# Convolution and gated feed-forward: lanes that convolve one unit ahead instead of two

## The chip, the cores and the metric

The kernel runs on one core of one Trainium2 chip. The metric is device time in microseconds of one execution. The core has five engines with queues of their own: PE (TensorE), DVE (VectorE), ACT (ScalarE), POOL (GpSimd) and SP (SyncE, which here issues DMAs and transposes). In the profile, PEld is TensorE's weight load, and a name such as POOLq is an engine's queue.

## The reference

The input x has 8 sequences of 4096 tokens with 192 channels, in float32. Each of 8 heads (24 channels) is convolved causally over 7 tokens with a softmax of 7 weights, and every token then passes a feed-forward layer of width 1536 with a product of two branches:

```python
w = softmax(weight)                                   # [8, 7], one set of taps per head
x_pad = concatenate([zeros(B, 6, D), x], axis=1)
y[b, s, h, :] = sum(w[h, k] * x_pad[b, s + k, h, :] for k in range(7))
y = y.reshape(B * S, 192)
out = (maximum(y @ w_gate, 0) * (y @ w_val)) @ w_out  # w_gate, w_val [192, 1536], w_out [1536, 192]
```

## The kernel before

Two sequences, b and b + 4, are handled side by side: one on partitions 0 to 63, the other on 64 to 127. The 192 channels are three groups c of 64. The work goes in 16 units u of 1024 tokens (of two sequences each), and each unit has two windows of 512 tokens.

A unit has two phases on TensorE. In the gate phase `gate_val(u, w)` is called for both windows. For each of 12 slices f of the width it issues six matmuls with Wg and six with Wv (L505), which read `xc[u]`, the convolved tokens. ScalarE takes the gate through a ReLU (L516, tile gr), and VectorE multiplies it by the value branch in PSUM (L517, tile hT). In the projection phase `project(u, ...)` multiplies hT by Wo for four outputs of 512 tokens each, i = 0 to 3, each in two turns of half height (`half_pass`, L539). The first unit uses matmuls of full height instead (`half_whole`, L559). `evict` copies each output out of PSUM (L576): ScalarE alone, and for i = 3 ScalarE and VectorE half each, except in unit 0. The PSUM pool has four buffers, used in turn, so the value matmuls of the second slice in a gate phase take the buffer that output i = 3 held.

The convolution is done in three ways:

- Unit 0: on TensorE with banded matrices, straight into `xc[0]` (`conv_dense`, L333).
- Unit 1: on TensorE too (`conv`, L358), in two calls of two parts, then copied by ScalarE to a tile y (L373) and transposed by DMAs of SP's queue into `xc[1]` (L395). The second call sits inside unit 0's projection.
- Units 2 to 15: "lanes". `lane_load` (L414) loads the tokens, `lane_turn` has GpSimd reorder them (L433, tile x_p) and SP's queue transpose them in nine DMAs (L436, tile x_r). Then each tap is a multiplication by a scalar per partition and an addition. Tokens 0 to 575 of the unit are VectorE's: ScalarE makes the first tap's product (`lane_first`, L469, tile acc), and VectorE accumulates the other six taps for three channel groups, 18 instructions (`lane_rest`, L481), of which the last three write `xc`. Tokens 576 to 1023 are made as 21 products (`product`, L452 on ScalarE, L454 on VectorE, tile prods), and GpSimd sums them in six adds (`add`, L458), the last of which writes `xc`. `VECTOR` lists the products (c, k) that VectorE makes; the rest are ScalarE's, spread over the four outputs of a projection (`work`, `cut`).

The order in each engine's queue is the order in which the program is written (`manual_schedule`); semaphores between engines are set by tile regions. In the loop over u, the products and accumulations for unit u + 2 are issued in unit u's projection, and the adds for unit u + 1 in unit u's gate phase, around `lane_turn(u + 2)` and `lane_load(u + 3)` in GpSimd's queue:

```python
lane = 1 <= u < NUNIT - 1
if lane:
    add(u + 1, 1)
...
if u + 2 < NUNIT:
    lane_first(u + 2)
    lane_rest(u + 2)
```

The tiles acc, prods and x_p have one buffer each, x_r two, xc three.

Of the kernel before, what the change touches and what calls it, by code (L numbers as in the profile page):

```python
# [15 lines left out]
def kernel(  # L16
# [23 lines left out]
    WIN = 512  # L40
    NWIN = S // WIN
    SUB = 112
    VECTOR = [
        [(0, 5), (1, 5), (2, 5), (0, 4), (1, 4), (2, 4), (2, 1)],
        [(0, 5), (1, 5), (2, 5), (0, 6), (2, 1)],
    ]
# [10 lines left out]
    GROUPS = [(0, [DSUB * j for j in range(GSUB)]), (0, [WIN + DSUB * j for j in range(GSUB)])]  # L57
    second = [min(t, 2 * UNIT - SUB) for t in range(UNIT, 2 * UNIT, SUB)]
    GROUPS += [(0, second[:GSUB]), (0, second[GSUB:])]
# [3 lines left out]
    xpool = ctx.enter_context(tc.tile_pool(name="xpool", bufs=3))  # L63
# [3 lines left out]
    ypool = ctx.enter_context(tc.tile_pool(name="ypool", bufs=2))  # L67
# [7 lines left out]
    def load_x(g):  # L75


        bp, toks = GROUPS[g]
        xt = xpool.tile([128, GSUB, 2, D], F16, name="x_h")
        rows, step = (SUB, DSUB) if g < 2 else (128, SUB)  # L80
        for st in range(2):
            b = bp + NB * st
            last = toks[-1] - toks[-2] != step
            n_full = len(toks) - int(last)
            src = bass.AP(
                tensor=x.tensor,
                offset=x.offset + (b * S + toks[0] - PAD) * D,
                ap=[[D, rows], [step * D, n_full], [1, D]],
            )
            nc.gpsimd.dma_start(out=xt[0:rows, 0:n_full, st, :], in_=src)  # L90
            if last:
                nc.gpsimd.dma_start(
                    out=xt[0 : SUB + PAD, len(toks) - 1, st, :],
                    in_=x[b, toks[-1] - PAD : toks[-1] + SUB, :],
                )
        return xt
# [208 lines left out]
    PLACE = {0: (0, 0, 0), 1: (0, 0, 1), 3: (0, 1, 0), 4: (0, 1, 1)}  # L305
    PLACE |= {6: (1, 0, 0), 7: (1, 0, 1), 2: (1, 1, 0), 5: (1, 1, 1)}

    def conv_dense(g, c):


        xt = xts[g]
        if g == 0 and c == 0:
            xc[0] = xcpool.tile([128, NCH, UNIT], F16, name="xc")
            both_halves(nc.vector.tensor_copy, 0, Wg)
            both_halves(nc.vector.tensor_copy, 0, Wv)
        t0 = GROUPS[g][1][0]
        rows = ROWS0
        ps = psum.tile([128, 2, 512], FP, name="ps")
        late = (1, 2, 3, 4, 0)
        both = [(jj, (0, 1)) for jj in late]  # L320
        if g == 0 and c == 0:
            both = [(jj, (st,)) for st in range(2) for jj in late[0:4]] + both[4:]
        for jj, sts in both:
            col = DSUB * jj
            n = min(DSUB, WIN - col)
            for second in range(2):
                for st in sts:
                    for k2 in range(2):
# [4 lines left out]
                        nc.tensor.matmul(  # L333
                            out=ps[p0 : p0 + m, 0, col : col + n],
                            lhsT=xt[0:rows, jj, st, 32 * k : 32 * k + m],
                            rhs=band(h)[0:rows, 0:n],
                            start=True,
                            stop=True,
                            tile_position=(0, p0),
                            skip_group_check=True,  # L340
                        )
# [3 lines left out]
    convs = {}  # L345

    def conv(g, part):


        xt = xts[g]  # L350
        bp, toks = GROUPS[g]
        n = len(toks)
        rows = SUB + PAD
        W = 2 * n * G
        ps = psum.tile([128, 2, 512], FP, name="ps")
        for h, (t, bank, slot) in PLACE.items():
            if t == part:
                nc.tensor.matmul(  # L358
                    out=ps[0:SUB, bank, W * slot : W * (slot + 1)],
                    lhsT=band(h),  # L360
                    rhs=xt[0:rows, 0:n, :, G * h : G * (h + 1)],
                    start=True,
                    stop=True,
                    skip_group_check=True,
                )
        if part == 0:
            convs[g] = ypool.tile([128, GSUB, NCH, 2, 64], F16, name="y")
        y = convs[g]

        def move(copy, bank, i0, step_in, c, r0, step_out, width):  # L370
            src = ps[0:SUB, bank, 0 : 2 * W]
            dst = y[0:SUB, 0:n, 0, :, 0:1]
            copy(  # L373
                out=bass.AP(
                    tensor=dst.tensor,
                    offset=dst.offset + 128 * c + r0,
                    ap=[dst.ap[0], [step_out, 2], [NCH * 128, n], [64, 2], [1, width]],
                ),
                in_=bass.AP(
                    tensor=src.tensor,  # L380
                    offset=src.offset + i0,
                    ap=[src.ap[0], [W + step_in, 2], [2 * G, n], [G, 2], [1, width]],
                ),
            )

        if part == 0:
            move(nc.scalar.copy, 0, 0, 0, 0, 0, G, G)
            move(nc.scalar.copy, 1, 0, 0, 1, 8, G, G)
            return
        move(nc.scalar.copy, 0, 0, 0, 2, 16, G, G)  # L390
        move(nc.scalar.copy, 1, 0, 8, 0, 48, 2 * 128 - 48, 16)
        move(nc.scalar.copy, 1, 16, -16, 1, 0, 56, 8)
        for jj, t in enumerate(toks):
            u, k = t // UNIT, min(SUB, UNIT - t % UNIT)
            nc.sync.dma_start_transpose(  # L395
                out=xc[u][:, :, t % UNIT : t % UNIT + k],
                in_=y[0:k, jj].rearrange("p c s r -> p (c s r)"),
            )
# [78 lines left out]
    def lane_rest(u):  # L477
# [11 lines left out]
        for c, k in VECTOR[u > 2]:  # L489
            product(nc.vector, u, c, k)  # L490
# [65 lines left out]
    def half_whole(h, st, outs):  # L556
        for q in range(4):
            for f in range(NFF):
                nc.tensor.matmul(  # L559
                    out=outs[q],  # L560
                    lhsT=h[:, f, st, 128 * q : 128 * (q + 1)],
                    rhs=Wo[:, f, :],
                    start=(f == 0),
                    stop=(f == NFF - 1),
                )

# [30 lines left out]
    def project(u, hs, work):  # L597
# [3 lines left out]
        if u == 0:  # L601
            order = [(i, 2) for i in range(4)]
        if u == NUNIT - 1:
            order = [(0, 0), (1, 0), (0, 1), (2, 0), (1, 1), (2, 3), (3, 0), (2, 4), (3, 1)]
        for i, turn in order:
            final = u == NUNIT - 1 and i == 3
            h, st = hs[i // 2], i % 2
            if turn in (0, 2):
                at[i] = slots(final)
            if turn in (1, 2):  # L610
                for c, k in work[i]:
                    product(nc.scalar, u + 2, c, k)
# [12 lines left out]
            if turn == 2:  # L625
                half_whole(h, st, at[i][1])
            else:
                done[i] = half_pass(h, st, at[i][1], final, turn, done.get(i))
            if turn:
                evict(at[i][0], (bp + NB * st) * S + WIN * (w0 + i // 2), final, u > 0 and i == 3)  # L630
            if u == 0 and i == 0:
                conv(3, 0)
                conv(3, 1)
# [9 lines left out]
    lane_load(2)  # L643
    xts[2] = load_x(2)
    nc.gpsimd.dma_start(out=Wo[:], in_=moe_w_out.rearrange("(c p) d -> p c d", p=128))
    for u in range(NUNIT):
        lane = 1 <= u < NUNIT - 1
        if lane:
            add(u + 1, 1)
        if u == 1:  # L650
            lane_load(3)
            add(2, 2)
            add(2, 3)
        hs = []
        if u == 0:
            hs.append(gate_val(0, 0))
        if u + 2 < NUNIT:
            lane_turn(u + 2)
        if u == 0:
            xts[3] = load_x(3)  # L660
        if 0 < u < NUNIT - 3:
            lane_load(u + 3)
        if lane:
            for k in range(4 if u == 1 else 2, KW - 1):
                add(u + 1, k)
        while len(hs) < 2:
            hs.append(gate_val(u, len(hs)))
        if lane:
            add(u + 1, KW - 1)
        if u == 0:  # L670
            xc[1] = xcpool.tile([128, NCH, UNIT], F16, name="xc")
            conv(2, 0)
            conv(2, 1)
        del xc[u]
        work = [[] for _ in range(4)]
        if u + 2 < NUNIT:
            lane_first(u + 2)
            lane_rest(u + 2)
# [35 lines left out]
```

## Time and profile before

| what | value |
|---|---|
| time, median of 3 runs | 768.64 us (768.06 to 768.94) |
| span of the profiled execution | 767.4 us |
| PE busy | 761.4 us, 99% |
| DVE busy | 692.2 us, 90% |
| ACT busy | 601.7 us, 78% |
| POOL busy | 369.9 us, 48% |
| L505 gate and value matmuls, mean of one | 376 ns, 4608 of them |
| L539 projection matmuls, mean of one | 243 ns, 5760 of them |
| L517 multiply on DVE | 1216 ns, 386 of them |
| L481 accumulation on DVE | 815 ns, 252 of them |
| L458 add on POOL | 3035 ns, 84 of them |

The profiler records a span from the first to the last instruction; a time of its own for the profiled execution is not given, and the median of the timed runs lies 1.2 us above that span. The share of an engine's busy time is an average over both phases of a unit. PE's matmuls overlap, since two of half height run at once and the next is issued before the last has ended, so a mean duration is not the distance from one to the next; for that the chain and the timeline are read. The granted TensorE clock is full in all 40 slices of the span.

### The profile page before, as it was taken

How to read it: one execution, taken by the hardware profiler on the slowest of the kernel's cores; microseconds unless marked ns; L12 is line 12 of the kernel's file. 1: busy time of each engine (PE TensorE's matmuls, PEld its weight loads, DVE VectorE, ACT ScalarE, POOL GpSimd, SP SyncE). 2: the span in 40 equal slices, each digit the busy share in tenths (PEclk: the TensorE clock that was granted, in tenths of full speed). 3: DMA queues.
4: the chain of work that ended last, by engine and by line, in shares of the span. 5: the costliest groups of instructions: out<-in, count | busy, mean ns of one | idle time of the engine just before them, and what ended most of it. 6: DMA issues, size and time to landing. Idle time of an engine off the chain costs nothing.

```text
span 767.4 us, 24881 instructions
## 1 busy us (share of the span) xinstructions
PE 761.4 (99%) x10842; PEld 502.1 (65%) x10842; DVE 692.2 (90%) x745; ACT 601.7 (78%) x736; POOL 369.9 (48%) x212
## 2 busy tenths in 40 slices
PE   9999999999999999999999999999999999999997
PEld 4495674946649476584855848567494674947657
DVE  7999999999999999999999999999999999995590
ACT  6797887878888788888878878788787887874671
POOL 8608648093570926619165290843809355080000
PEclk9999999999999999999999999999999999999999
DMA  8956727180462705428064271722719131200202
GB/s 121 138 97 118 91 90 88 54 122 6 100 78 69 107 23 98 59 85 94 26 112 43 85 91 44 109 28 89 89 50 110 21 95 37 65 21 23 63 2 85
DMA packets 131827, 56.13 MB, mean 73 GB/s; under 512 B 96757, under 2 KB 131717, under 8 KB 131717
## 3 DMA queue, kind: packets, MB, share of 16 engines
q1 hardware_dynamic: 90805, 38.85, 24.9%
q0 software_dynamic: 40768, 15.59, 18.8%
q8 instruction: 85, 1.39, 0.8%
q14 instruction: 25, 0.20, 0.1%
q10 hardware_dynamic: 144, 0.10, 0.0%
HBM read 31.68 MB, written 25.17 MB: 74 GB/s over the span
## 4 chain that ended last, share of the span: by engine, by line
PE 99%; DMA 1%; issue 0%; DVE 0%; POOL 0%; POOLq 0%
PE ps L505 65%; PE ps L539 31%; PE ps L559 2%; DMA x_h<-in_x_dram 1%; PE ps L333 0%; PE ps L358 0%; DVE acc L576 0%; POOL spaced L129 0%; POOLq L698 0%
## 5 line engine op out<-in xcount | busy, mean ns | idle before, releaser
L517 DVE TENSOR_TENSOR hT<-gr,ps 128x1024 f16<-128x1024 f16 (+1 forms) x386 | 469.0, 1216 | 36.9 <-ACT gr L516 9.9
L516 ACT ACTIVATE gr<-ps 128x1024 f16<-128x1024 f32 (+1 forms) x386 | 393.3, 1020 | 101.9 <-PE ps L505 100.1
L458 POOL TENSOR_TENSOR prods<-prods 128x1344 f32<-128x1344 f32 x70 | 212.5, 3035 | 309.8 <-DVE prods L454 306.4
L505 PE MATMUL ps<-xc,Wg 64*128 64x512 f16 x2304 | 311.9, 376 | 0.0
L505 PE MATMUL ps<-xc,Wv 64*128 64x512 f16 x2304 | 311.8, 376 | 0.0
L539 PEld LDWEIGHTS <-hT 64*128 64x128 f16 x5760 | 238.0, 94 | 3.6
L539 PE MATMUL ps<-Wo,hT 64*128 64x192 f16 x5760 | 240.1, 243 | 0.0
L505 PEld LDWEIGHTS <-Wv 64*128 64x128 f16 x2304 | 129.6, 94 | 118.7 <-DVE hT L517 0.3
L505 PEld LDWEIGHTS <-Wg 64*128 64x128 f16 x2304 | 112.2, 94 | 132.5 <-issue 0.5
L481 DVE SCALAR_TENSOR_TENSOR acc<-x_r,tap,acc 128x576 f32<-128x576 f16 x210 | 154.3, 815 | 1.6 <-DMA x_r<-x_p 1.6
L452 ACT ACTIVATE prods<-x_r,tap 128x448 f32<-128x448 f16 x222 | 130.4, 664 | 0.0
L576 ACT COPY out_s<-ps 128x768 f32<-128x768 f32 (+1 forms) x64 | 46.2, 722 | 53.9 <-PE ps L539 44.0
L414 POOL DMA_DIRECT2D x_e<-in_x_dram x56 | 45.2, 818 | 3.3 <-POOL x_p L433 3.3
L433 POOL COPY x_p<-x_e 128x1728 f16<-128x1728 f16 x28 | 44.8, 1627 | 1.5 <-DMA x_e<-in_x_dram 1.5
L458 POOL TENSOR_TENSOR xc<-prods 128x1344 f16<-128x1344 f32 x14 | 42.4, 3026 | 1.1
L481 DVE SCALAR_TENSOR_TENSOR xc<-x_r,tap,acc 128x576 f16<-128x576 f16 x42 | 31.8, 816 | 0.0
L469 ACT ACTIVATE acc<-x_r,tap 128x576 f32<-128x576 f16 x42 | 29.4, 768 | 0.0
L454 DVE TENSOR_SCALAR prods<-x_r,tap 128x448 f32<-128x448 f16 x72 | 27.4, 452 | 0.0
L576 DVE COPY out_s<-ps 128x384 f32<-128x384 f32 x14 | 7.8, 556 | 14.8 <-ACT out_s L576 14.8
L559 PE MATMUL ps<-Wo,hT 128*128 128x192 f16 x192 | 16.2, 246 | 0.0
L559 PEld LDWEIGHTS <-hT 128*128 128x128 f16 x192 | 15.9, 98 | 0.0
L576 DVE COPY acc<-ps 128x192 f32<-128x192 f32 x1 | 0.4, 358 | 14.2 <-PE ps L539 14.2
(52 smaller groups left out, 62.6 us busy)
## 6 DMA issues: line engine op xcount, KB each, us to landing
out_dram<-out_s SPq DMA_DIRECT2D x62, 384.0 KB
x_e<-in_x_dram POOLq DMA_DIRECT2D x34, 192.0 KB, 6.2
x_e<-in_x_dram POOLq DMA_DIRECT2D x22, 240.0 KB, 5.0
x_r<-x_p SPq DMA_TRANSPOSE x126
Wo<-in_moe_w_out_dram POOLq DMA_DIRECT2D x1, 576.0 KB
x_h<-in_x_dram POOLq DMA_DIRECT2D x2, 240.0 KB, 7.3
x_h<-in_x_dram POOLq DMA_DIRECT2D x2, 210.0 KB, 4.7
x_h<-in_x_dram POOLq DMA_DIRECT2D x2, 192.0 KB, 7.7
```

Source lines behind the costliest of these rows:

```text
L414: nc.gpsimd.dma_start(out=xe[:, j : j + n, st, :, :].rearrange("p j c r -> p j (c r)"), in_=bass.AP(tensor=x.tensor, offset=x.offset + (b ...
L433: nc.gpsimd.tensor_copy(out=xp[:, :, :, st, :], in_=xe[:, :, st, :, :])
L452: engine.activation(out=out, in_=in_, func=ACTF.Copy, scale=scale)
L458: nc.gpsimd.tensor_tensor(out=pr[:, 0] if k < KW - 1 else xc[u][:, :, LDVE:UNIT], in0=pr[:, 0], in1=pr[:, k], op=ALU.add,)
L469: nc.scalar.activation(out=accs[u][:, c, :], in_=shifted(u, c, 0, 0), func=ACTF.Copy, scale=tap[:, c, 0:1],)
L481: nc.vector.scalar_tensor_tensor(out=xc[u][:, c, 0:LDVE] if k == KW - 1 else acc[:, c, :], in0=shifted(u, c, k, 0), scalar=tap[:, c, k : k ...
L505: nc.tensor.matmul(out=pss[i][:, st, :], lhsT=W[64 * st : 64 * st + 64, c, 128 * f : 128 * (f + 1)], rhs=xcb[64 * st : 64 * st + 64, c, WI ...
L516: nc.scalar.activation(out=gr[:, sts], in_=pss[0][:, sts], func=ACTF.Relu)
L517: nc.vector.tensor_tensor(out=h[:, f, sts], in0=gr[:, sts], in1=pss[1][:, sts], op=ALU.mult)
L539: mm = nc.tensor.matmul(out=outs[q], lhsT=h[64 * r : 64 * r + 64, f, st, 128 * q : 128 * (q + 1)], rhs=Wo[64 * r : 64 * r + 64, f, :], sta ...
L559: nc.tensor.matmul(out=outs[q], lhsT=h[:, f, st, 128 * q : 128 * (q + 1)], rhs=Wo[:, f, :], start=(f == 0), stop=(f == NFF - 1),)
L576: one(out=dst[:, step * j : step * j + step], in_=src[:, step * j : step * j + step])
```

## The change

The lanes now make unit u + 1 in unit u, not unit u + 2, and unit 1 is made by them as well. `conv` and its tile y are gone, with the loads of x for it; `half_whole` is gone, so that unit 0 projects as the others do, and its last output too is copied by ScalarE and VectorE. All six adds stand behind `project` in the program, so that in GpSimd's queue they follow `lane_turn(u + 1)` and `lane_load(u + 2)` and wait only for the products. `VECTOR` is one list of five products; the product (2, 1) goes to ScalarE and (1, 6) to VectorE.

```diff
-    VECTOR = [
-        [(0, 5), (1, 5), (2, 5), (0, 4), (1, 4), (2, 4), (2, 1)],
-        [(0, 5), (1, 5), (2, 5), (0, 6), (2, 1)],
-    ]
+    VECTOR = [(0, 5), (1, 5), (2, 5), (0, 6), (1, 6)]
...
-    xpool = ctx.enter_context(tc.tile_pool(name="xpool", bufs=3))
+    xpool = ctx.enter_context(tc.tile_pool(name="xpool", bufs=2))
...
-    ypool = ctx.enter_context(tc.tile_pool(name="ypool", bufs=2))
...
-    def conv(g, part):
...
-        for c, k in VECTOR[u > 2]:
+        for c, k in VECTOR:
             product(nc.vector, u, c, k)
...
-    def half_whole(h, st, outs):
...
     def project(u, hs, work):
...
-        if u == 0:
-            order = [(i, 2) for i in range(4)]
...
-                    product(nc.scalar, u + 2, c, k)
+                    product(nc.scalar, u + 1, c, k)
...
-                evict(at[i][0], (bp + NB * st) * S + WIN * (w0 + i // 2), final, u > 0 and i == 3)
-            if u == 0 and i == 0:
-                conv(3, 0)
-                conv(3, 1)
+                evict(at[i][0], (bp + NB * st) * S + WIN * (w0 + i // 2), final, i == 3)
...
-    lane_load(2)
-    xts[2] = load_x(2)
+    lane_load(1)
     nc.gpsimd.dma_start(out=Wo[:], in_=moe_w_out.rearrange("(c p) d -> p c d", p=128))
     for u in range(NUNIT):
-        lane = 1 <= u < NUNIT - 1
-        if lane:
-            add(u + 1, 1)
-        if u == 1:
-            lane_load(3)
-            add(2, 2)
-            add(2, 3)
+        lane = u + 1 < NUNIT
         hs = []
         if u == 0:
             hs.append(gate_val(0, 0))
+        if lane:
+            lane_turn(u + 1)
         if u + 2 < NUNIT:
-            lane_turn(u + 2)
-        if u == 0:
-            xts[3] = load_x(3)
-        if 0 < u < NUNIT - 3:
-            lane_load(u + 3)
-        if lane:
-            for k in range(4 if u == 1 else 2, KW - 1):
-                add(u + 1, k)
+            lane_load(u + 2)
         while len(hs) < 2:
             hs.append(gate_val(u, len(hs)))
-        if lane:
-            add(u + 1, KW - 1)
-        if u == 0:
-            xc[1] = xcpool.tile([128, NCH, UNIT], F16, name="xc")
-            conv(2, 0)
-            conv(2, 1)
         del xc[u]
         work = [[] for _ in range(4)]
-        if u + 2 < NUNIT:
-            lane_first(u + 2)
-            lane_rest(u + 2)
+        if lane:
+            lane_first(u + 1)
+            lane_rest(u + 1)
             todo = [(c, k) for k in (0, 1, 2, 3, 4, 6) for c in range(NCH)]
-            todo = [ck for ck in todo if ck not in VECTOR[u > 0]]
-            cut = [0, 4, 8, 12, 16] if u == 0 else [0, 5, 10, 15, 16]
-            work = [todo[a:b] for a, b in zip(cut, cut[1:])]
+            todo = [ck for ck in todo if ck not in VECTOR]
+            work = [todo[a:b] for a, b in zip([0, 5, 10, 15], [5, 10, 15, 16])]
         project(u, hs, work)
+        if lane:
+            for k in range(1, KW):
+                add(u + 1, k)
```

More of the change, by code (lines that the diff above doesn't have):

```diff
@@ L56 @@
     TDVE = (LDVE + HALO) // 128
-    GROUPS = [(0, [DSUB * j for j in range(GSUB)]), (0, [WIN + DSUB * j for j in range(GSUB)])]
-    second = [min(t, 2 * UNIT - SUB) for t in range(UNIT, 2 * UNIT, SUB)]
-    GROUPS += [(0, second[:GSUB]), (0, second[GSUB:])]
+    STARTS = [[DSUB * j for j in range(GSUB)], [WIN + DSUB * j for j in range(GSUB)]]
     ctx.enter_context(tc.manual_schedule())
     const = ctx.enter_context(tc.tile_pool(name="const", bufs=1))
-    xpool = ctx.enter_context(tc.tile_pool(name="xpool", bufs=3))
+    xpool = ctx.enter_context(tc.tile_pool(name="xpool", bufs=2))
     epool = ctx.enter_context(tc.tile_pool(name="epool", bufs=1))
@@ L75, in load_x @@
     def load_x(g):
-        bp, toks = GROUPS[g]
         xt = xpool.tile([128, GSUB, 2, D], F16, name="x_h")
-        rows, step = (SUB, DSUB) if g < 2 else (128, SUB)
         for st in range(2):
-            b = bp + NB * st
-            last = toks[-1] - toks[-2] != step
-            n_full = len(toks) - int(last)
             src = bass.AP(
                 tensor=x.tensor,
-                offset=x.offset + (b * S + toks[0] - PAD) * D,
-                ap=[[D, rows], [step * D, n_full], [1, D]],
-            )
[L90 to L95, printed above, removed]
+                offset=x.offset + (NB * st * S + STARTS[g][0] - PAD) * D,
+                ap=[[D, SUB], [DSUB * D, GSUB], [1, D]],
+            )
+            nc.gpsimd.dma_start(out=xt[0:SUB, :, st, :], in_=src)
         return xt
@@ L301 @@
     xc = {}
-    PLACE = {0: (0, 0, 0), 1: (0, 0, 1), 3: (0, 1, 0), 4: (0, 1, 1)}
-    PLACE |= {6: (1, 0, 0), 7: (1, 0, 1), 2: (1, 1, 0), 5: (1, 1, 1)}
     def conv_dense(g, c):
@@ L315, in conv_dense @@
             both_halves(nc.vector.tensor_copy, 0, Wv)
-        t0 = GROUPS[g][1][0]
+        t0 = STARTS[g][0]
         rows = ROWS0
@@ L343, in conv_dense @@
         copy(out=xc[0][:, c, t0 : t0 + WIN], in_=ps[:, 0, :])
-    convs = {}
-    def conv(g, part):
[L350 to L398, printed above, removed]
     xes, xrs, accs, prods = {}, {}, {}, {}
@@ L554, in half_pass @@
             return done
-    def half_whole(h, st, outs):
[L557 to L565, printed above, removed]
     def put(copy, queue, src, row, n, gap, os_=None):
@@ L607, in project @@
             h, st = hs[i // 2], i % 2
-            if turn in (0, 2):
+            if turn == 0:
                 at[i] = slots(final)
-            if turn in (1, 2):
+            if turn == 1:
                 for c, k in work[i]:
-                    product(nc.scalar, u + 2, c, k)
+                    product(nc.scalar, u + 1, c, k)
             if turn > 2:
@@ L624, in project @@
                 continue
[L625 to L628, printed above, removed]
+            done[i] = half_pass(h, st, at[i][1], final, turn, done.get(i))
             if turn:
-                evict(at[i][0], (bp + NB * st) * S + WIN * (w0 + i // 2), final, u > 0 and i == 3)
-            if u == 0 and i == 0:
-                conv(3, 0)
-                conv(3, 1)
+                evict(at[i][0], (bp + NB * st) * S + WIN * (w0 + i // 2), final, i == 3)
     for c in range(NCH):
```

## The prediction

> **What bounds the kernel now.** I read the page's chain first, then the timeline of one unit in the middle of the run, then the groups behind it.
>
> ```profile
> PE 99%; DMA 1%; issue 0%; DVE 0%; POOL 0%; POOLq 0%
> by line: PE ps L505 64.9%; PE ps L539 31.0%; PE ps L559 2.1%; DMA x_h<-in_x_dram 0.7%; PE ps L333 0.4%; PE ps L358 0.2%; issue 0.1%; DVE acc L576 0.0%; POOL spaced L129 0.0%; POOLq L698 0.0%
> ```
>
> TensorE never waits: the span is its work. So an edit gains only what it takes from TensorE, and loses all by which it makes TensorE wait. In the same chain every later unit is 31.08 us of gate and value matmuls (L505) and 15.84 us of projection (L539), 46.92 us in all. The timeline of one projection, with P = 230.94 us for its start:
>
> ```profile
> 228.96 3.81 DVE L517 TENSOR_TENSOR hT<-gr,ps 128x1024 f16<-128x1024 f16 x3
> 230.94 16.00 PE L539 MATMUL ps<-Wo,hT 64*128 64x192 f16 x384
> 232.69 11.02 DVE L481 SCALAR_TENSOR_TENSOR acc<-x_r,tap,acc 128x576 f32<-128x576 f16 x15
> 237.78 2.91 ACT L452 ACTIVATE prods<-x_r,tap 128x448 f32<-128x448 f16 x5
> 241.74 2.90 ACT L452 ACTIVATE prods<-x_r,tap 128x448 f32<-128x448 f16 x5
> 243.63 2.27 DVE L481 SCALAR_TENSOR_TENSOR xc<-x_r,tap,acc 128x576 f16<-128x576 f16 x3
> 245.82 1.90 DVE L454 TENSOR_SCALAR prods<-x_r,tap 128x448 f32<-128x448 f16 x5
> 246.78 0.81 PE L505 MATMUL ps<-xc,Wg 64*128 64x512 f16 x6
> 247.63 0.55 DVE L576 COPY out_s<-ps 128x384 f32<-128x384 f32 x1
> 247.89 3.03 POOL L458 TENSOR_TENSOR prods<-prods 128x1344 f32<-128x1344 f32 x1 [21.72 <-DVE prods L454]
> ```
>
> The columns are start, length, engine, line, tiles and count. VectorE is busy through the whole projection: 18 accumulations (L481) from P+1.75, 0.735 us apart, five products, and half an eviction that ends at P+17.24. GpSimd stands idle until all of that is done. Its adds (L458) run only in the gate phase, beside the multiplies L517:
>
> ```profile
> L458 POOL TENSOR_TENSOR prods<-prods x70: 3018/3028/3098, 60.7 to 682.6; 128x1344 f32<-128x1344 f32 x70
> L481 DVE SCALAR_TENSOR_TENSOR acc<-x_r,tap,acc x210: 809/814/821, 44.8 to 665.2; 128x576 f32<-128x576 f16 x105
> L517 DVE TENSOR_TENSOR hT<-gr,ps x19: 1220/1221/1223, 201.8 to 225.1; 128x1024 f16<-128x1024 f16 x19
> L517 DVE TENSOR_TENSOR hT<-gr,ps x24: 1220/1221/1223, 699.5 to 745.1; 128x1024 f16<-128x1024 f16 x24
> ```
>
> The last two lines are the multiplies with adds beside them (201 to 226 us) and with GpSimd idle (700 to 746): no nanosecond of difference. But a multiply has one operand in SBUF (gr), the other in PSUM. An accumulation has two in SBUF (x_r, acc), and none of the 252 in this trace runs beside an add.
>
> **The change, part by part.**
>
> *TensorE's convolution of the second unit goes.* In the chain its two pieces are 0.99 and 0.82 us: 1.81 us gained. Its ten ScalarE copies, ten transposes on SP's queue and six GpSimd loads go too; nothing waited for them. The first unit's projection turns from 192 whole-height matmuls (3.96 + 11.88 = 15.84 us) into 384 half-height ones, 15.84 us in every other unit: nothing.
>
> *One more unit goes through the lanes.* Unit 1's takes in unit 0's projection the place that unit 2's had. There VectorE had waited 1.63 us for x_r (44.79 us) and the projection now starts 0.9 us sooner, at about 41.4; the chain ends 44.79 + 15.5 = 60.3 us, TensorE wants it at 41.4 + 17.8 = 59.2: 1.1 us lost once if x_r lands no sooner, 0 if it does. I take 1.1.
>
> *The lanes lose a unit of lead.* The next unit's first gate matmul now waits for xc that VectorE writes in the projection just before it, its second window for GpSimd's last add. Undisturbed, the first third of xc is there at P+13.5 (243.63 + 0.81) and is wanted at P+15.84; the last third is there at P+14.96 and is wanted four matmuls later, at about P+16.3. The half eviction, behind the five products in VectorE's order, frees the PSUM buffer of the fourth value matmul group: there at P+17.24, wanted at P+17.78 (248.72 us). So the margin is 0.54 us, and every later microsecond of VectorE is one of TensorE.
>
> *GpSimd's queue.* The adds move from the gate phase into the projection: the product (2,1) that held the first one back is now ScalarE's, first of its second five, done at about P+7.5. Adds 1 to 4 need ScalarE's products alone, all there by P+13.7; add 5 needs three of VectorE's, add 6 the last two. Moved behind them are the two turns (L433, 3.2 us), four loads (3.3 us) and, through these, the nine transposes on SP's queue (12.2 us). Undisturbed, six adds take 18.5 us and end at P+26, window 1 opens at P+31.4, and x_r lands at about P+43, before the next projection at P+46.9. All of that is covered, by 5.4 and by 4 us.
>
> *The unknown: an add beside an accumulation.* At P+7.5 the eighth accumulation runs and ten are to come. Bounds: the multiplies say 0 per add; two engines that take strict turns cost VectorE a whole add each, 3.03 us. I take the upper end, because the multiply's row differs in the one thing that matters, the second SBUF operand, and because GpSimd is short of reads itself: its add takes 2.25 ns an element with two operands, its copy x_p 0.94 with one (1629 ns for 1728). With turns, add 1 runs at P+7.65, one accumulation, add 2, one, add 3, one, add 4, then seven: four adds, 12.1 us. Add 5 arrives while the fourth product runs and holds back the fifth. A product is one SBUF operand, but it takes 0.38 us for 448 elements, 0.85 ns each against 1.19 in the multiply and 1.28 in the accumulation: faster than one stream gives on this engine, so it too seems to use a second path. 0 or 3.03; I take 3.03.
>
> The Trainium skill (SBUF — State Buffer, section Who interferes with whom) has a rule against this change: a VectorE instruction with two SBUF inputs contends with a GpSimd instruction that reads SBUF, and the later one waits until the other has finished. No run yet shows it; by it the sum is the one that I take, by the multiplies' row it would be 767.9.
>
> VectorE then ends 5 x 3.03 = 15.15 us later, and TensorE waits 15.15 - 0.54 = 14.6 us in each of 15 units. Nothing gives it back: in the gate phase TensorE needs 1.295 us for each of 24 steps and VectorE 1.22, so behind the wait TensorE sets the pace again. GpSimd is done at about P+35 and the next projection starts at P+61.5, so x_r is in time.
>
> *TensorE after a wait.* It stands from P+15.8 to P+25.7, and again for 4 us. At the program's start it issued its 512-column matmuls every 0.425 us for 3 us, later every 0.216; after 0.64 us of idleness at 5.3 us it was not slow. So 0 to 1.5 us per unit; I take 0, as the waits inside a unit are nearer to the short idleness, and keep 15 x 1.5 = 22 us for the range. The Trainium skill (TensorE: Matmul & The Clock Gate, Part 1) says that the clock halves after about 3.4 us of idleness for about as long; by that rule an estimate of 1.7 us per unit would make it 1012. The trace shows half speed only at the start.
>
> Sum, against the profiled span of 767.4 us (the median of 768.64 has 1.2 us more around it): -1.8 + 1.1 + 15 x 14.6 = +218, so 768.6 + 218 = 987 us. Without add 5's cost it is 15 x 11.6 = 174, 942; with the slow restart 1009.
>
> **Rivals.**
>
> *The adds wait, not VectorE.* Accumulations start every 0.735 us and last 0.814, so they overlap, and GpSimd may find no gap. Then add 1 starts at about P+15 (behind the accumulations) or P+16.7 (behind the products), six take 18.5 us, and window 1, due at P+31.4, opens at P+33.6 to P+35.3: 2.2 to 3.9 us a unit, 33 to 59 us, 801 to 827. For it: the overlap. Against it: a read that ends before its instruction leaves a gap.
>
> *They share.* Both slow down, and VectorE loses half an add each: 6 to 7.5 us, less 0.54, 15 times: 850 to 873. For it: an add at 2.25 ns an element can't fill a path at every cycle. Against: nothing in the trace shows a half-slowed row.
>
> *No collision.* Adds and accumulations run as adds and multiplies do. Then only 1.8 us of TensorE go, less 0 to 1.1: 766.8 to 767.9. It decides as long as VectorE loses under 0.54 us a unit, 0.13 us per overlapped add; the multiplies speak for it, the second operand against.
>
> That the change does not do what it says can be left out: in the built order the first gate matmuls wait for VectorE in three steps, and those of window 1 for GpSimd.
>
> **How the numbers follow.** Turns 0.58, sharing 0.12, waiting adds 0.18, no collision 0.12. The forecast's own range is 942 to 1009. The range leaves out only no collision: from 800, the waiting adds' lower end, to 1015, slow restarts included. About 0.2% (1.5 us) is what a measurement of this kernel can tell from no change. The first three cases are slower: 0.88. No collision is split evenly by unit 0's loss: faster 0.06, same 0.06.
>
> **What would show it.** Right: L481 in the projection with a few instructions of about 3.8 us, or gaps of 3 us in VectorE there; TensorE waiting some 10 us for xc and 4 us for the eviction at each unit's start; units of 61.5 us; about 15 us of projection-phase GpSimd work. Waiting adds: L481 at 814 ns, L458 lengthened, the wait in front of window 1 on GpSimd. Wrong: both lines as before and TensorE still at 99%. Slower restarts would show as the gate phase longer than 31.08 us, free of waits.

## The result and the profile after

The changed kernel takes 856.72 us (median of 5 runs, 856.23 to 858.11) against 768.64: the ratio is 1.1146, with a 95% interval of 1.1134 to 1.1159. That is 88 us slower, where the forecast had 218. The sign was right. The engine that is late was not: the forecast had TensorE wait for VectorE, and it waits for GpSimd. The case that came is the rival in which the adds wait, and one term that the forecast took as zero is added to it.

The page of the changed kernel: the granted clock, the chain, and two groups (busy time and mean ns of one, idle time before them and what ended it).

```profile
PEclk9998999989999899998999989999899998999989
...
PE 75%; POOL 11%; issue 9%; DMA 2%; SPq 1%; ACT 1%; POOLq 0%; DVE 0%; ACTq 0%
...
L384 POOL TENSOR_TENSOR prods<-prods 128x1344 f32<-128x1344 f32 x75 | 361.2, 4816 | 281.9 <-ACT prods L378 277.1
...
L431 PE MATMUL ps<-xc,Wg 64*128 64x512 f16 x2304 | 334.8, 395 | 55.0 <-POOL xc L384 55.0
```

Where TensorE was 99% of the chain, it is 75%; GpSimd and the "issue" time around its adds stand in for the rest. TensorE waits 55.0 us for `xc`, all of it for GpSimd's part and none for VectorE's. The clock, full in every slice before, is below 0.9 in eight of the 40 slices. The adds (now L384) have a mean of 4.8 us instead of 3.03. The next view tells where that mean is from: the lines of the adds and of the accumulations (now L407) over the whole run, as min/median/max ns.

```profile
L384 POOL TENSOR_TENSOR prods<-prods x75: 3018/3025/12067, 50.0 to 810.7; 128x1344 f32<-128x1344 f32 x75
L407 DVE SCALAR_TENSOR_TENSOR acc<-x_r,tap,acc x225: 808/812/816, 43.0 to 793.6; 128x576 f32<-128x576 f16 x113
```

No accumulation is touched (816 ns at most, 821 before), nor a product of VectorE (L380, 453 ns at most). The adds are unchanged in the median, but the longest takes 12.07 us, and that is the first one of a unit. The timeline of one projection, P = 200.23 us:

```profile
200.23 16.01 PE L465 MATMUL ps<-Wo,hT 64*128 64x192 f16 x384
201.98 11.02 DVE L407 SCALAR_TENSOR_TENSOR acc<-x_r,tap,acc 128x576 f32<-128x576 f16 x15
207.83 24.48 POOL L384 TENSOR_TENSOR prods<-prods 128x1344 f32<-128x1344 f32 x5 [19.15 <-ACT prods L378]
212.92 2.27 DVE L407 SCALAR_TENSOR_TENSOR xc<-x_r,tap,acc 128x576 f16<-128x576 f16 x3
215.11 1.90 DVE L380 TENSOR_SCALAR prods<-x_r,tap 128x448 f32<-128x448 f16 x5
...
232.39 3.01 POOL L384 TENSOR_TENSOR xc<-prods 128x1344 f16<-128x1344 f32 x1
...
235.45 1.46 PE L431 MATMUL ps<-xc,Wg 64*128 64x512 f16 x6 [3.67 <-POOL xc L384]
```

Five adds with no gap take 5 x 3.03 + 4 x 0.08 = 15.5 us; here they take 24.48. Add 1 is let go at P+7.60, inside the run of accumulations, and ends 12.06 us later, at 219.89 us. An add's own length of 3.02 us back from there is 216.87, when VectorE's last product was just ending (215.11 + 1.90 = 217.01): as if it had begun only then. From there six adds in a row end at P+35.2. TensorE could have begun window 1 at P+31.4 (24 groups of six matmuls, 0.6475 us apart, from 216.07 us) and is 3.84 us late.

That is not all of the loss: the six matmuls behind the wait take 1.46 us instead of 0.82. Windows of time around the same wait, TensorE alone (length, busy time and matmuls, granted clock, DMA share, GB/s):

```profile
core 0: us, PE busy (x), PEclk, DMA share, GB/s
229.20:235.45 6.25, 2.58 (x24) 0.98 0.00 0
235.45:236.50 1.05, 1.05 (x6) 0.50 0.00 0
...
237.50:238.50 1.00, 1.00 (x8) 0.50 0.00 0
238.50:239.50 1.00, 1.00 (x12) 0.92 0.00 0
239.50:240.50 1.00, 1.00 (x14) 1.00 0.48 98
```

In finer windows of this trace the granted clock is 0.50 from 235.25 to 238.66 us, 3.2 us of it behind the wait. In the next unit it is 0.50 from 286.45 to 293.27 us, 5.5 us of it behind a wait as long (3.66 us), and so in turn through the run. In the chain, the 144 matmuls that follow take 17.28 or 18.4 us, in turn from unit to unit, instead of the 15.72 that the same piece takes at full clock (`e11_fill`, below):

```profile
235.45 17.28 PE ps L431 x144
...
287.77 18.41 PE ps L431 x144
```

So a unit loses 3.84 us to the adds and 1.6 or 2.7 us to the clock. Units of 46.92 us have become 52.3 and 53.4 us.

### The profile page after: what moved, and what is told of

It is laid out like the page before. It is cut to its first block, busy times and chain, and to the rows that moved or that the text cites. A ratio compares the mean times of both kernels' runs of the same rounds, so it can differ in the third digit from the quotient of the medians.

```text
span 854.5 us, 25310 instructions
## 1 busy us (share of the span) xinstructions
PE 795.2 (93%) x11018; PEld 526.5 (62%) x11018; DVE 706.5 (83%) x767; ACT 609.4 (71%) x747; POOL 523.9 (61%) x218
## 4 chain that ended last, share of the span: by engine, by line
PE 75%; POOL 11%; issue 9%; DMA 2%; SPq 1%; ACT 1%; POOLq 0%; DVE 0%; ACTq 0%
PE ps L431 50%; PE ps L465 25%; POOL xc L384 5%; POOL prods L384 5%; SPq L362 1%; DMA x_e<-in_x_dram 1%; DMA Wg<-in_moe_w_gate_dram 1%; ACT prods L378 1%; DMA x_r<-x_p 0%; POOLq L600 0%; POOL Wg L164 0%; POOL Wg L157 0%; POOL x_e L340 0%; ACT out_s L491 0%; POOL Wv L157 0%
## 5 line engine op out<-in xcount | busy, mean ns | idle before, releaser
L384 POOL TENSOR_TENSOR prods<-prods 128x1344 f32<-128x1344 f32 x75 | 361.2, 4816 | 281.9 <-ACT prods L378 277.1
L431 PE MATMUL ps<-xc,Wg 64*128 64x512 f16 x2304 | 334.8, 395 | 55.0 <-POOL xc L384 55.0
L431 PE MATMUL ps<-xc,Wv 64*128 64x512 f16 x2304 | 331.5, 391 | 0.0
L465 PEld LDWEIGHTS <-hT 64*128 64x128 f16 x6144 | 254.3, 94 | 3.5
L465 PE MATMUL ps<-Wo,hT 64*128 64x192 f16 x6144 | 256.2, 243 | 0.0
L431 PEld LDWEIGHTS <-Wg 64*128 64x128 f16 x2304 | 128.5, 98 | 191.0 <-issue 80.6
L431 PEld LDWEIGHTS <-Wv 64*128 64x128 f16 x2304 | 138.5, 97 | 125.0 <-issue 19.0
L407 DVE SCALAR_TENSOR_TENSOR acc<-x_r,tap,acc 128x576 f32<-128x576 f16 x225 | 165.3, 812 | 0.0
L378 ACT ACTIVATE prods<-x_r,tap 128x448 f32<-128x448 f16 x240 | 140.7, 660 | 1.5 <-DMA x_r<-x_p 1.5
L384 POOL TENSOR_TENSOR xc<-prods 128x1344 f16<-128x1344 f32 x15 | 45.2, 3011 | 1.2
L407 DVE SCALAR_TENSOR_TENSOR xc<-x_r,tap,acc 128x576 f16<-128x576 f16 x45 | 34.1, 812 | 0.0
L395 ACT ACTIVATE acc<-x_r,tap 128x576 f32<-128x576 f16 x45 | 31.4, 765 | 0.3 <-DMA x_r<-x_p 0.3
L380 DVE TENSOR_SCALAR prods<-x_r,tap 128x448 f32<-128x448 f16 x75 | 28.5, 448 | 0.0
L141 PE MATMUL ps<-const-bfloat16-1.0 128*128 128x512 bf16 (+1 forms) x10 | 4.2, 560 | 0.9 <-PEq L589 0.9
```

The source lines that it names most:

```text
L378: engine.activation(out=out, in_=in_, func=ACTF.Copy, scale=scale)
L380: engine.tensor_scalar(out=out, in0=in_, scalar1=scale, scalar2=None, op0=ALU.mult)
L384: nc.gpsimd.tensor_tensor(out=pr[:, 0] if k < KW - 1 else xc[u][:, :, LDVE:UNIT], in0=pr[:, 0], in1=pr[:, k], op=ALU.add,)
L395: nc.scalar.activation(out=accs[u][:, c, :], in_=shifted(u, c, 0, 0), func=ACTF.Copy, scale=tap[:, c, 0:1],)
L407: nc.vector.scalar_tensor_tensor(out=xc[u][:, c, 0:LDVE] if k == KW - 1 else acc[:, c, :], in0=shifted(u, c, k, 0), scalar=tap[:, c, k : k ...
L431: nc.tensor.matmul(out=pss[i][:, st, :], lhsT=W[64 * st : 64 * st + 64, c, 128 * f : 128 * (f + 1)], rhs=xcb[64 * st : 64 * st + 64, c, WI ...
```

## The experiments

Left as a question was why the adds wait, when the forecast had them take turns with VectorE, and whether lateness of the adds and the clock are all of the loss.

**How many adds: `e6_short`, `e3_four`, `e2_five`, `e4_seven`.** After, with most of the accumulations left out, or with fewer or more adds behind `project`.

```diff
 e6_short, in lane_rest
-        for k in range(1, KW):
+        for k in (KW - 1,):
 the other three, behind project
-            for k in range(1, KW):
+            for k in (1, 2, 5, 6):            # e3_four
+            for k in (1, 2, 4, 5, 6):         # e2_five
+            for k in (1, 2, 3, 3, 4, 5, 6):   # e4_seven
```

> As after, with 15 of the 18 accumulations of each unit left out (only the last tap's three are left, so the convolution lacks five taps in tokens 0 to 575). Theory (VectorE's run holds the add): VectorE is through by P+6, the first add takes 3.03 us at P+7.5, six end at P+26, TensorE does not wait, 766 to 769 us. Rival (ScalarE's products or the DMAs lengthen the first add): still 12 us, still 850 to 860 us.

> As after, with the adds of taps 3 and 4 left out. The four adds end at about P+29, window 1 is due at P+31.4: no wait, no half speed, 766 to 768 us, which would also be what the change gains where nothing waits (1.8 us of TensorE less up to 1.1 us in the first unit). Rival (VectorE's xc or its eviction is late too): 775 us or more.

> As after, with the add of tap 3 left out (five adds a unit, that tap is missing in tokens 576 to 1023). The adds end 3.09 us sooner, so TensorE's wait in front of window 1 falls from 3.84 to 0.75 us. If half speed follows only a wait of several microseconds: 766.8 + 15 x 0.75 = 778 us, gate phases otherwise 31.1 us. If each wait costs the same 1.7 to 2.9 us of half speed: some 811 us. If the waits of after are not the adds' doing: no change, 857 us.

> As after, with the add of tap 3 made twice (seven adds a unit). TensorE waits 6.9 us in front of window 1 instead of 3.84: 857 + 46 = 903 us if the half speed behind it stays as it is (1.7 to 2.9 us lost per unit), up to 915 if a longer wait makes it longer. Rival (a wait below some bound is caught up by the PSUM buffers): under 890 us.

Measured: 766.53 us without the 15 accumulations (ratio to before 0.9962, 0.9948 to 0.9976), 767.49 with four adds (0.9991, 0.9981 to 1.0), 779.42 with five (1.0148, 1.0126 to 1.0169) and 901.4 with seven (1.1733, 1.1714 to 1.1753); six are 856.72. All four are as expected. The loss needs both the long run on VectorE and more than four adds behind it. With four adds the last one is early enough and nothing is lost. From six to seven the time rises by 44.7 us, 3.0 us in each of 15 units: one add. With five, TensorE's waits are 9.3 us in 15 units, 1.1 us at most, and the mean granted clock is 0.999: so short a wait doesn't lower it. The first two runs also show what the change gains where nothing waits: 0.7 to 2.3 us against the runs of before beside them (768.20 and 768.86).

**The release: `e1_hold`.** The product (2,1) is VectorE's last again and (1,6) ScalarE's, so that add 1 isn't let go before VectorE is done.

```diff
-    VECTOR = [(0, 5), (1, 5), (2, 5), (0, 6), (1, 6)]
+    VECTOR = [(0, 5), (1, 5), (2, 5), (0, 6), (2, 1)]
```

> As after, but the product (2, 1) is VectorE's last again, and (1, 6) ScalarE's, so that the first add is released at about P+16.7 instead of P+7.5. Theory (it can't run before then anyway): 853 to 861 us, first add 3.03 us long. Rival (the add makes headway beside the accumulations): later adds, 15 times up to 3 us more, up to 900 us.

Measured: 857.78 us, ratio 1.1152 (1.1133 to 1.1172), no different from after. The timeline of one unit, GpSimd:

```profile
325.76 15.44 POOL L384 TENSOR_TENSOR prods<-prods 128x1344 f32<-128x1344 f32 x5 [27.18 <-DVE prods L380]
```

Five adds in 15.44 us, none of them long, and yet the same time. The early release bought next to nothing (TensorE waits for GpSimd 60.0 us in all, against 55.0 in after): the 12.07 us of add 1 are 9 us of waiting and 3.02 of work.

**The collision by itself: `p1_probe`, `p2_probe`.** Kernels of stages: the same accumulations, products and adds, with nothing else of the reference.

> Not the reference's computation: only rows of instructions in the shapes of the kernel, in nine stages, each with its parts alone or against each other. Theory (a dense run of VectorE instructions that use the second SBUF path keeps GpSimd out until the run ends): 18 accumulations 815 ns each with and without adds; the first of four adds that come in mid-run is as long as the rest of the run plus 3.03 us; the same behind a dense run of 30 products; not behind multiplies with a PSUM operand nor behind accumulations whose sum lies in PSUM (adds at once, 3.03 us each). Where the adds come first, the first accumulation waits for the end of one add (up to 3 us). With a PSUM copy of 0.55 us between accumulations an add gets in, and the accumulation behind it takes some 3 us longer. Rival (strict turns, the forecast): adds get in between dense accumulations, accumulations of 3.8 us. Rival (something else lengthened the first add, ScalarE's writes or a DMA): all adds here 3.03 us, everywhere.

> Not the reference's computation: rows of instructions as in the first probe. There GpSimd's fill of 3.5 us ended right before its first add, and adds and accumulations took turns (accumulations of 3.56 us), which is not what the changed kernel shows; here GpSimd stands idle before its first add, as it does in the kernel, and ScalarE lets it go at four places in a run of 18 accumulations. Theory A (an add that comes to a running chain of accumulations from idleness waits for the chain's end; one that stands right behind other work of GpSimd gets its turn): first add up to 10 us long, accumulations all 0.81 us, in all four places; with a short fill or copy in front of the first add the turns come back (accumulations of 3.56 us) or only behind that copy's own wait. Theory B (idleness does not matter, something else in the kernel holds the add): turns in all stages, accumulations of 3.56 us and first adds of 3.4 us.

The timeline of the first: 18 accumulations alone, then 18 into which four adds fall.

```profile
17.89 13.21 DVE L88 SCALAR_TENSOR_TENSOR acc<-x_r,tap,acc 128x576 f32<-128x576 f16 x18 [2.15 <-ACT tap L55]
...
47.59 24.23 DVE L88 SCALAR_TENSOR_TENSOR acc<-x_r,tap,acc 128x576 f32<-128x576 f16 x18 [16.48 <-ACT tap L55]
...
51.45 13.92 POOL L97 TENSOR_TENSOR prods<-prods 128x1344 f32<-128x1344 f32 x4
```

These are the forecast's turns: four adds lengthen VectorE's run by 24.23 - 13.21 = 11.0 us, 2.75 us for each, and an accumulation that meets one takes 3.56 us. Products take turns too: one that meets an add takes 3.20 us instead of 0.45. Multiplies with one operand in PSUM do not, as the trace of before had it, nor do accumulations that read their sum from PSUM (18 of them of 128x512 in 11.94 us, 744 ns each, beside adds at 3.02 us). The expectation that a dense run keeps GpSimd out was missed. In the second probe GpSimd is idle before the first add, and the add falls at four places within an accumulation: turns in all four. So neither idleness nor the phase is what separates kernel and probe. But one stage of it is held as in the kernel: a run of 30 products, the first add let go at the 7th.

```profile
178.88 10.97 DVE L127 TENSOR_SCALAR vec<-x_r,tap 128x448 f32<-128x448 f16 x30 [2.75 <-ACT vec L55]
181.40 20.58 POOL L97 TENSOR_TENSOR prods<-prods 128x1344 f32<-128x1344 f32 x4 [12.44 <-ACT prods L55]
```

**The lead: `e5_lead`, `e8_lead_turn`.** Before, two units ahead, but with the six adds behind the projection as in after, and the product that held the first one back given to ScalarE; in the second also with `lane_turn` and `lane_load` a unit earlier.

```diff
 e5_lead
-        if lane:
-            add(u + 1, 1)
...
+        if u + 2 < NUNIT:
+            for k in range(1, KW):
+                add(u + 2, k)
 e8_lead_turn, beside that
-        if u + 2 < NUNIT:
-            lane_turn(u + 2)
...
+        elif u + 3 < NUNIT:
+            lane_turn(u + 3)
```

> The kernel before, two units ahead and with TensorE's convolution, but with the adds behind the projection in which their products are made, and the product that held back the first add given to ScalarE, as in after. Theory (the cost is the lost lead, not the place of the adds): the first add is 12 us long here too, but a unit of lead covers it: 768 to 771 us. Rival (adds beside accumulations cost in themselves, by VectorE or a slower TensorE): 800 us or more.

> As the run with a unit of lead and the adds behind the projection (801.9 us), but each unit's turn stands one unit earlier in GpSimd's queue, ahead of the adds. Theory (there the late x_r cost 33 us, since the turns stood behind adds that were held for 12 us; the lost lead alone is what costs in the change): first add still some 12 us, x_r in time, 768 to 772 us. Rival (adds that are held cost in another way too): 785 us or more.

Measured: 801.89 us (1.042, 1.0401 to 1.0439) and 788.07 (1.0251, 1.0234 to 1.0268). Both totals miss, and lie where the expectations had put the rivals; the traces tell why. In the first, the held adds stand in GpSimd's queue ahead of the turn of the unit that VectorE needs next: ScalarE waits 33.1 us in 11 units for x_r. With the turn moved ahead of them that is gone: from the gate phase at 122.66 us to the one at 735.24, 13 units take 47.1 us each against before's 46.92, though add 1 is held there as well (12.07 us at most). So with a unit of lead the held adds cost next to nothing. Most of the rest is lost before that: the projection at 153.74 us stands at 137.26 in the chain of before. It goes in unit 0, whose timeline has the other behaviour:

```profile
46.66 23.97 DVE L481 SCALAR_TENSOR_TENSOR acc<-x_r,tap,acc 128x576 f32<-128x576 f16 x15 [3.92 <-ACT acc L469]
49.95 4.04 POOL L433 COPY x_p<-x_e 128x1728 f16<-128x1728 f16 x2 [12.82 <-DMA xc<-y]
```

Here GpSimd gets in, and VectorE's 15 accumulations take 23.97 us instead of 11.02. The kernel can do both.

**What decides: `e9_copy_first`, `p3_probe`.** In the first, a GpSimd copy is let go ahead of add 1, as in that unit 0; in the second, the kernel's neighbours are put beside the accumulations one by one.

```diff
         if lane:
+            nc.gpsimd.tensor_copy(out=spare[:], in_=prods[u + 1][:, 1])
             for k in range(1, KW):
```

> After, with one more GpSimd instruction per unit: a copy of the first tap's products (128x1344, from float32 to float16, into a tile that nobody reads) ahead of the first add, released by the same products. If a copy that comes first lets GpSimd take turns with the accumulations, as it did in the first unit of the run before this one, the forecast's own size is seen in the kernel: accumulations of some 3.5 us, VectorE 12 to 17 us late per unit, 950 to 1010 us. If a copy is held like an add, it ends behind VectorE's products and pushes the six adds back by its own 1.3 to 1.6 us: 15 times that on 856.7, 875 to 882 us, with accumulations of 814 ns.

> Rows only: no part of the reference is computed. Seven stages, each with 18 accumulations as in the kernel (or, in stage 1 to 7, what is added to them), into whose run two adds of GpSimd are let go some 5 us after its start, GpSimd idle before. Stage 1: nothing beside. 2: ScalarE makes dense products beside. 3: five products of VectorE stand behind the accumulations. 4: two multiplies with PSUM in front, the five products behind, and ScalarE dense. 5: 512-column matmuls on TensorE beside. 6: all of it. 7: all of it, and a GpSimd copy let go first, the adds behind it. The stage that holds what keeps an add out in the kernel shows its first add at about 10 us and accumulations of 0.81 us; every other shows an add of 3.0 to 3.6 us and accumulations of about 3.6 us. Theory A (what else runs on the core decides): 1 in turns, 6 held, and 2, 3, 4 or 5 names the part. Theory B (the kind of GpSimd instruction that comes first decides): 6 held and 7 in turns. If 6 shows turns, neither of these is the cause.

Measured: 882.22 us (one run), with accumulations of 818 ns at most: the copy is held like an add (10.37 us in the unit at 322 us), so its kind doesn't matter. In the probe six stages of seven take turns, those with TensorE, multiplies and products beside among them, and the one with all of it; only stage 2, with ScalarE's products, is held. Its lines, and those of GpSimd in stage 7, where a copy comes first:

```profile
37.58 13.21 DVE L88 SCALAR_TENSOR_TENSOR acc<-x_r,tap,acc 128x576 f32<-128x576 f16 x18 [2.56 <-ACT tap L55]
42.90 13.85 POOL L97 TENSOR_TENSOR prods<-prods 128x1344 f32<-128x1344 f32 x2 [17.24 <-ACT prods L124]
...
155.92 1.92 POOL L161 COPY x_p<-x_e 128x1728 f16<-128x1728 f16 x1 [17.92 <-ACT x_e L55]
161.03 6.70 POOL L97 TENSOR_TENSOR prods<-prods 128x1344 f32<-128x1344 f32 x2 [3.19 <-ACT prods L124]
```

Stages 4 and 6 have the same dense ScalarE and take turns, so ScalarE is not the reason. What stage 2 has alone is a late release: 5.32 us after the run's start, in its 8th accumulation. In all others the first release falls in the 4th. In the first probe it was the 6th at the latest, in unit 0 of `e8_lead_turn` the 5th; in the kernel, wherever an add was held, it is the 8th or a later one.

**The place in the run: `p4_probe`, `e10_early`.** The probe lets the add go later and later. In the kernel, ScalarE's first portion gets one product more, so that add 1 is let go 1.6 us earlier.

```diff
-            work = [todo[a:b] for a, b in zip([0, 5, 10, 15], [5, 10, 15, 16])]
+            work = [todo[a:b] for a, b in zip([0, 6, 11, 16], [6, 11, 16, 16])]
```

> Rows only: no part of the reference is computed. Nine stages that let GpSimd's first add into an unbroken run of VectorE at different places. 1 to 3: 18 accumulations, ScalarE otherwise idle, the add let go some 3.8, 4.9 and 6.0 us after the run's start (in its 6th, 7th and 9th instruction). 4 to 6: the same with ScalarE's dense products, some 3.6, 4.2 and 4.8 us (5th, 6th, 7th). 7 and 8: 30 products, the add let go in the 4th to 6th. 9: 24 accumulations, one add let go in the 4th, the second some 9 accumulations after it. Theory C (how far VectorE's unbroken run has come decides; the rows so far: 6th instruction or earlier, turns; 7th product, 8th accumulation or later, held): turns in 1, 4, 5, 7, 8 (add 3.0 to 3.6 us, accumulation or product 3.2 to 3.6), held in 3 (10 us) and in 9's second add, with the border in 2 and 6. Theory A (ScalarE's dense products beside decide): turns in 1 to 3, held in 4 to 6. If it is the time of the release within an accumulation, or neither, the pattern is another, as 3 in turns or 4 held.

> After, with six products in ScalarE's first portion instead of five (six, five, five and none), so that the first add is let go 1.6 us earlier, some 4.3 us after VectorE's run begins instead of 5.85: in its 6th accumulation. Theory C: the add gets in and takes turns, as the forecast had it for after; four to six adds then cost VectorE about 3 us each, accumulations of some 3.5 us are seen, and the time is 930 to 1010 us. If the place in the run is not what decides: the adds are held as before, 855 to 860 us.

The timeline of the probe: stage 2, stage 3, and stage 9.

```profile
37.58 18.72 DVE L88 SCALAR_TENSOR_TENSOR acc<-x_r,tap,acc 128x576 f32<-128x576 f16 x18 [2.56 <-ACT tap L55]
42.46 6.67 POOL L97 TENSOR_TENSOR prods<-prods 128x1344 f32<-128x1344 f32 x2 [15.35 <-ACT prods L55]
...
58.86 13.21 DVE L88 SCALAR_TENSOR_TENSOR acc<-x_r,tap,acc 128x576 f32<-128x576 f16 x18 [2.56 <-ACT tap L55]
64.83 13.20 POOL L97 TENSOR_TENSOR prods<-prods 128x1344 f32<-128x1344 f32 x2 [15.71 <-ACT prods L55]
...
184.01 3.18 POOL L97 TENSOR_TENSOR prods<-prods 128x1344 f32<-128x1344 f32 x1 [13.62 <-ACT prods L55]
194.32 10.21 POOL L97 TENSOR_TENSOR prods<-prods 128x1344 f32<-128x1344 f32 x1 [7.13 <-ACT prods L55]
```

An add let go 4.88 us into the run (stage 2, 7th accumulation) costs VectorE 5.5 us for two; one let go at 5.97 us (stage 3, the 9th) waits for all of it, and VectorE's 13.21 us are those of a run alone. ScalarE's products change nothing: stages 4 to 6, at 3.65, 4.21 and 4.77 us, all take turns (18.75 us). In products the 4th and the 5th let it in, the 7th had not. In stage 9 the first add gets in, and the second, which comes after nine more accumulations, is held for the rest of the same run. The count begins anew behind a turn: in stage 7 of the third probe the copy took its turn in the 4th accumulation, and the add let go in the 9th, five later, got in (3.21 us). In the kernel, the timeline of a unit (P = 331.36 us):

```profile
333.12 22.11 DVE L407 SCALAR_TENSOR_TENSOR acc<-x_r,tap,acc 128x576 f32<-128x576 f16 x15
337.38 13.59 POOL L384 TENSOR_TENSOR prods<-prods 128x1344 f32<-128x1344 f32 x4 [23.64 <-ACT prods L378]
355.16 2.26 DVE L407 SCALAR_TENSOR_TENSOR xc<-x_r,tap,acc 128x576 f16<-128x576 f16 x3
```

Add 1 comes 4.26 us into the run instead of 5.85 and is let in. Four adds lengthen the 15 accumulations from 11.02 to 22.11 us, TensorE waits for VectorE (121.4 us in all) and for GpSimd only once (4.1 us), and the kernel takes 932.94 us (one run). That is the forecast's mechanism, one product of ScalarE away. In unit 0 of the same run the release falls in the 8th accumulation, and there the add is held, 12.32 us.

**The clock: `e11_fill`.** After, with 14 matmuls between the two windows that keep TensorE at work while it waits.

```diff
         xcb = xc[u]
+        if w == 1 and u > 0:
+            fill = psum.tile([128, 2, 512], FP, name="ps")
+            for _ in range(14):
+                nc.tensor.matmul(out=fill[:, 0, :], lhsT=Wg[:, 0, 0:128], rhs=xcb[:, 0, 0:WIN], start=True, stop=True)
```

> After, with 14 more matmuls of 512 columns on TensorE between the two windows of each unit from 1 on, into a PSUM buffer that nobody reads: 3.0 us at full clock, less than TensorE's wait of 3.7 to 3.8 us there. If the 2.3 us per unit that are lost behind the wait are the clock that an idle TensorE is granted, they go: 856.7 - 15 x 2.3 = 822 us (818 to 828), the wait for xc at 0.5 to 1 us, L431 at 376 to 380 ns. If they have another cause (the order of the buffers, the multiplies behind), 850 to 860 us or more.

Measured: 824.34 us, ratio to before 1.0722 (1.0699 to 1.0745). The waits and the chain:

```profile
PE ps L435 <- POOL xc L384: 8.4, 15, 0.7
```

```profile
330.08 15.72 PE ps L435 x144
...
380.85 15.72 PE ps L435 x144
```

More work on the engine that waits makes the kernel 32 us faster, 2.2 us in each of 15 units. The mean granted clock is 1.00, and a unit is 380.85 - 330.08 = 50.77 us: 46.92 and the 3.85 us by which the adds are late, nothing else.

## Why the prediction was right and wrong

The accounts close: 766.5 to 767.5 us where nothing waits, + 15 x 3.84 = 58 us for the adds (824.34 without the clock's part), + 32 us for the clock: 857.

- *Direction.* Slower, by the lost lead and by an add that meets an accumulation: right, and `e8_lead_turn` shows from the second unit on that held adds cost next to nothing as long as there is a unit of lead.
- *The failed step* is "I take the upper end": strict turns from P+7.65 on, by which VectorE ends 15.15 us later and TensorE waits for it. Instead no accumulation got longer than 816 ns, add 1 waited until P+16.6, and TensorE waited 55.0 us for GpSimd and not at all for VectorE. Part of what the forecast reasoned is so: the second operand in SBUF makes the collision, products collide too, and the multiplies don't. But it took for granted that a waiting add gets in at the next change of instruction. From the 8th accumulation on it does not, and add 1 was let go in the 9th. The case needed the place in VectorE's run at which the add is let go, and no row of before could give the border.
- *The rival* "the adds wait, not VectorE" had the mechanism and the times: add 1 at P+16.7, window 1 open at P+35.3, against P+16.6 and P+35.2 measured. Its upper end of 827 us and the clock's 32 make 859, against 856.72. Its reason, that overlapping accumulations leave no gap, is not enough: early in the same run the add finds one.
- *Mis-sized: the restart.* It was taken as 0 with 1.5 us as its bound. It is 1.6 or 2.7 us a unit, 2.2 in the mean by `e11_fill`. The forecast leaned on a short idleness of 0.64 us, though its own sum had TensorE stand for 9.9 us; the wait that came is 3.67 us. The Trainium skill (TensorE: Matmul & The Clock Gate, Part 1) has the half clock after about 3.4 us of idleness; this trace agrees, with 0.50 behind 3.67 us, and a mean of 0.999 where waits are 1.1 us at most. The half clock lasts 3.4 us in one unit, as the forecast read that page, and 6.8 us in the next. The forecast's estimate by that page, 1.7 us a unit, was nearer than its own number.
- *Mis-sized: a turn.* It costs 2.75 to 2.77 us and not 3.03. In `e10_early` four adds cost VectorE a turn each. The fifth, which the forecast had hold back the last product, is let go in the fourth product and waits 0.44 us for the end of VectorE's run, which it does not lengthen (five products in 1.89 us). So even with turns the forecast was high: 932.94 against 987, or 942 with four adds of 3.03 us.
- *TensorE's convolution*, 1.8 us gained less up to 1.1: the two runs without a wait are 0.7 and 2.3 us below before. Right within their spread.
- *The rule of the Trainium skill* (SBUF — State Buffer, section Who interferes with whom), that the later of the two waits until the other has finished, is seen in both behaviours. What the runs add to it is that a late add waits for VectorE's whole run and not for one instruction.

Open is why the border lies at the 8th accumulation: no run shows more than its place, and for products it lies between the 5th and the 7th instruction. Why the half clock lasts 3.4 us in one unit and 6.8 in the next, behind waits of the same length, is open too. No version with all the adds and accumulations is faster than before, and what there is to gain without a wait is some 2 us.

## What to carry to other kernels

Before work is moved into a phase in which another engine is in a dense run, find out which of the two waits there, since the same collision cost 88 us in one order and 164 in another, and the moment at which the first moved instruction is let go decided it. Work with a unit of lead can be late for free, so count what a lost lead uncovers, and let the turns of the next unit stand ahead of adds that may be held. Where TensorE must wait for several microseconds, price the wait with its clock: here a wait of 3.8 us cost 6.

## What the runs showed of the hardware

- A GpSimd add (or copy) that reads SBUF and is let go in the 8th or a later of a run of accumulations is held until the run is over, so that an add of 3.02 us takes up to 12.5, at no cost to VectorE; let go in the 7th or earlier, it takes turns, and an accumulation of 0.81 us takes 3.56. Behind a turn the count begins anew: an add let go in the 9th, five accumulations behind a copy's turn, got in.
- A product with one SBUF operand (0.45 us, 128x448) collides with an add as an accumulation does. An accumulation that reads its sum from PSUM does not: 744 ns beside adds of 3.02 us.
- TensorE's granted clock is 0.50 for 3.2 or 5.5 us, in turn, behind a wait of 3.67 us, and 0.999 in the mean of a run with waits of 1.1 us at most.
